# Exchanging the DMA queues of loads and stores in an attention backward kernel: paired dV and dK stores to GpSimd, K and V loads to SyncE

## The chip, the cores and the metric

One NeuronCore of a Trainium2 chip. The metric is the device time of one execution in microseconds (us). The kernel is already tuned. Its time before the change is 1880.39 us, the median of three runs (1872.74 to 1903.6). Later comparisons use runs of both kernels on the same chip in the same rounds. The record calls a run slow when it lies over 1.5% above the fastest run of the same kernel, and fast otherwise. Ratios use fast runs alone; medians are over all runs.

In the profile lines PE is TensorE, PEld its loading of weights, DVE VectorE, ACT ScalarE, POOL GpSimd and SP SyncE. A q behind an engine's name (SPq) means its sequencer, which issues its DMAs. SBUF is the on-chip memory that DMAs fill, and PSUM the one that TensorE writes, in banks. A DMA lands when its completion is reported. A ring is the queue in which one issuer's DMAs stand.

## The reference, cut to what matters

Two independent attention blocks (A and B) with cached K and V run forward and backward in one program. Each has batch 8, 96 queries, 32 heads, 512 keys and head size 128, in bfloat16. The program returns the output and the gradients of x, k_cache, v_cache, wq and wo of both blocks.

```python
q = (x @ wq).reshape(B, Sq, H, Dh).transpose(0, 2, 1, 3)
scores = einsum("bhqd,bhkd->bhqk", q, k_cache) * Dh ** -0.5
p = softmax(scores)
o = einsum("bhqk,bhkd->bhqd", p, v_cache)
out = o.transpose(0, 2, 1, 3).reshape(B, Sq, H * Dh) @ wo
# and jax.vjp of it: dx, dK, dV, dwq, dwo
```

The large data are K and V, which are read once, and dK and dV, which are written once: 512 (head, batch) pairs in all, 128 KB each for K, V, dK and dV.

## The kernel before

A software pipeline runs one (head, batch) pair, a "tick", at a time. K and V arrive for two ticks at once. V is also needed transposed (VT). A transposing DMA from SBUF to SBUF makes it. dV and dK leave PSUM through ScalarE, one tick at a time, into three SBUF buffers each, and SyncE stores them.

```python
OFF = dict(ld=-1, vt=1, s1=2, s2=3, s3=3, s4=4, s5=5, s6=7, s7=8, s8=9)   # stage -> tick

def c_ld(h, b):          # every second tick: 256 KB of V, 256 KB of K, issued by GpSimd
    K_sb = kvp.tile([128, 2, KC, 128], BF16, name="K_sb", bufs=7)
    V_sb = kvp.tile([128, 2, KC, 128], BF16, name="V_sb", bufs=5)
    nc.gpsimd.dma_start(V_sb[:], vc[b:b + 2, h].rearrange("b (p c) d -> p b c d", c=KC))
    nc.gpsimd.dma_start(K_sb[:], kc[b:b + 2, h].rearrange("b (p c) d -> p b c d", c=KC))

def c_vt(h, b):          # every second tick: 256 KB, SBUF to SBUF, issued by SyncE
    VT = kvp.tile([128, 2 * KC, 128], BF16, name="VT", bufs=4)
    nc.sync.dma_start_transpose(VT[:], CS[(blk, h, b)]["V2"][:].rearrange("p a c d -> p (a c d)"))

def c_s4(h, b):          # every tick; c_s7 does the same for dK
    dV_ps = bank([128, KC * 128], F32, "dV_ps")
    ...                  # four matmuls
    dV_sb = wk.tile([128, KC * 128], BF16, name="dV_sb", bufs=3)
    nc.scalar.activation(dV_sb[:], dV_ps[:], ACT.Identity, scale=1.0)
    nc.sync.dma_start(dv[b, h].rearrange("(p c) d -> p (c d)", c=KC), dV_sb[:])
...
ps=P(name="ps", bufs=8, space=PSUM)      # eight PSUM banks, shared by all
stp=P(name="stp", bufs=5)                # staging of block B's inputs
```

GpSimd also computes (P_sb and prod, once a tick each) and issues the DMAs of the weights and their gradients.

Of the kernel before, what the change touches and what calls it, by code (L numbers as in the profile page):

```python
# [53 lines left out]
def build_block(tc, em, tick0, blk, x, kc, vc, wq, wo, g_all, out_all, dx, dk, dv, dwq, dwo, ident, ones, pools, HG=8, first=True, groups=None):  # L54
    nc = tc.nc
# [40 lines left out]

    S = {}
    G = {}
    HS = pools["HS"]
    CS = pools["CS"]  # L100

# [127 lines left out]
    def c_ld(h, b):  # L229
        def f():  # L230
            K_sb = kvp.tile([128, 2, KC, 128], BF16, name="K_sb", bufs=7)
            V_sb = kvp.tile([128, 2, KC, 128], BF16, name="V_sb", bufs=5)
            nc.gpsimd.dma_start(V_sb[:], vc[b:b + 2, h].rearrange("b (p c) d -> p b c d", c=KC))
            nc.gpsimd.dma_start(K_sb[:], kc[b:b + 2, h].rearrange("b (p c) d -> p b c d", c=KC))  # L234
            for i in range(2):
                CS[(blk, h, b + i)] = dict(K_sb=K_sb[:, i], V_sb=V_sb[:, i], V2=V_sb)
        return f
# [104 lines left out]
    def c_s4(h, b):  # L342
        def f():
            st = CS[(blk, h, b)]
            hs = HS[(blk, h)]
            P_sb = st["P_sb"]
            dV_ps = bank([128, KC * 128], F32, "dV_ps")
            for c in range(KC):
                nc.tensor.matmul(dV_ps[:, c * 128:(c + 1) * 128], P_sb[:, c * 128:(c + 1) * 128], hs["dOnat_h"][:, b * 128:(b + 1) * 128], start=True, stop=True)  # L349
            dV_sb = wk.tile([128, KC * 128], BF16, name="dV_sb", bufs=3)  # L350
            nc.scalar.activation(dV_sb[:], dV_ps[:], ACT.Identity, scale=1.0)  # L351
            nc.sync.dma_start(dv[b, h].rearrange("(p c) d -> p (c d)", c=KC), dV_sb[:])
        return f

    def c_s5b(h, b):
        def f():
            st = CS[(blk, h, b)]
            hs = HS[(blk, h)]
            tok = slice(b * Sq, (b + 1) * Sq)
            prod = wk.tile([128, Sq], BF16, name="prod", bufs=4)  # L360
            nc.gpsimd.tensor_tensor(prod[:], hs["OT_h"][:, tok], hs["dOT_h"][:, tok], op=ALU.mult)  # L361
            st["prod"] = prod
        return f
# [13 lines left out]
    def c_s7(h, b):  # L377
        def f():
            st = CS[(blk, h, b)]
            hs = HS[(blk, h)]  # L380
            dS_sb = st["dS_sb"]
            dK_ps = bank([128, KC * 128], F32, "dK_ps")
            for c in range(KC):
                nc.tensor.matmul(dK_ps[:, c * 128:(c + 1) * 128], dS_sb[:, c * 128:(c + 1) * 128], hs["Qnat_h"][:, b * 128:(b + 1) * 128], start=True, stop=True)  # L384
            dK_sb = wk.tile([128, KC * 128], BF16, name="dK_sb", bufs=3)
            nc.scalar.activation(dK_sb[:], dK_ps[:], ACT.Identity, scale=1.0)  # L386
            nc.sync.dma_start(dk[b, h].rearrange("(p c) d -> p (c d)", c=KC), dK_sb[:])
        return f

    def qA(h, which):  # L390
# [97 lines left out]
    for g in range(NG):  # L488
        h0 = GH0[g]
        for hh in range(groups[g]):  # L490
            h = h0 + hh
            c0t = tick0 + h * B
            em.add(c0t + HK["pA"], SL_LOAD, pA(h))
            em.add(c0t + HK["pB"], SL_HEAD, pB(h))
            for si in range(NTS):
                em.add(c0t + HK["pC0"][min(si, len(HK["pC0"]) - 1)], SL_HEAD, pC(h, 0, si))
                em.add(c0t + HK["pC1"][min(si, len(HK["pC1"]) - 1)], SL_HEAD, pC(h, 1, si))
            em.add(c0t + HK["pD1"], SL_HEAD, pD(h, 1))
            em.add(c0t + HK["pD0"], SL_HEAD, pD(h, 0))
            for b in range(B):  # L500
                ct = c0t + b
                if b % 2 == 0:
                    em.add(ct + OFF["ld"], SLOTS["LOAD"], c_ld(h, b))
                    em.add(ct + OFF["vt"], SLOTS["LOAD"] + 1, c_vt(h, b))
                em.add(ct + OFF["s2"], SLOTS["S2A"], c_s2a(h, b))
                em.add(ct + OFF["s2"], SLOTS["S2B"], c_s2b(h, b))
                em.add(ct + OFF["s3"], SLOTS["S3A"], c_s3a(h, b))
                em.add(ct + OFF["s3"], SLOTS["S3B"], c_s3b(h, b))
                em.add(ct + OFF["s5"], SLOTS["S5B"], c_s5b(h, b))
                em.add(ct + OFF["s4"], SLOTS["S4"], c_s4(h, b))  # L510
                key = (blk, h, b)
                for table, stages in ((KD, ("s1", "s7", "s6")), (OD, ("s8", "s5", "s4"))):
                    for i, stage in enumerate(stages):
                        table.setdefault(ct + OFF[stage], [None] * 3)[i] = key
                em.add(ct + OFF["s6"], SLOTS["S6"], c_s6(h, b))
                em.add(ct + OFF["s7"], SLOTS["S7"], c_s7(h, b))
            em.add(c0t + HK["qA0"], SL_HEAD, qA(h, 0))
            for di in range(len(dsplits)):
                em.add(c0t + HK["qB"][min(di, len(HK["qB"]) - 1)], SL_HEAD + 1, qB(h, di))
            em.add(c0t + HK["qA1"], SL_HEAD, qA(h, 1))  # L520
            qd_parts = HK["qD"]
            for (k_, c_lo, c_hi) in qd_parts:
                if c_lo < DC:
                    em.add(c0t + k_, SL_HEAD + 2, qD(h, c_lo, min(c_hi, DC)))
        cLg = tick0 + (h0 + groups[g] - 1) * B + B - 1
        gs0 = max(3, (GSPREAD0 * groups[g]) // HG)
        gs1 = max(3, (GSPREAD1 * groups[g]) // HG)
        em.add(cLg + OFF["s5"] - 2, SL_LOAD, gW(g))
        subs = [(0, t, gi) for t in range(TT) for gi in range(len(gsplits))] + [(1, t, gi) for t in range(TT) for gi in range(len(gsplits))]
        n_out = TT * len(gsplits)  # L530
        for i, (which, t, gi) in enumerate(subs):
            if which == 0:
                tk = cLg + OFF["s5"] + 2 + (i * gs0) // n_out
            else:
                tk = cLg + OFF["s8"] + 2 + gs0 - 3 + ((i - n_out) * gs1) // n_out
            em.add(tk, SL_GRP, gU(g, which, t, gi))
# [5 lines left out]
def _kernel_impl(tc, A_x, A_k_cache, A_v_cache, A_wq, A_wo, B_x, B_k_cache, B_v_cache, B_wq, B_wo, grad_out,  # L542
           out_0, out_1, out_2, out_3, out_4, out_5, out_6, out_7, out_8, out_9, out_10, HG=8, slots=None, off=None, hk=None, ev=None, gspread=None, groupsA=None, groupsB=None):
    global GSPREAD0, GSPREAD1
    nc = tc.nc
    if slots:
        SLOTS.update(slots)
    if off:
        OFF.update(off)
    if hk:  # L550
        HK.update(hk)
    if ev:
        EV.update(ev)
    if gspread:
        GSPREAD0, GSPREAD1 = gspread
    with ExitStack() as ctx:
        P = lambda **kw: ctx.enter_context(tc.tile_pool(**kw))
        cst = P(name="gconst", bufs=1)
        ident = cst.tile([128, 128], BF16, name="ident")
        make_identity(nc, ident[:])  # L560
        ones = cst.tile([128, 1], BF16, name="ones")
        nc.vector.memset(ones[:], 1.0)
        pools = dict(
            const=P(name="const", bufs=1),
            ps=P(name="ps", bufs=8, space=PSUM),
            kvp=P(name="kv", bufs=11),
            wk=P(name="wk", bufs=3),
            hd=P(name="hd", bufs=2),
            hst=P(name="hst", bufs=HG + 2),
            grp=P(name="grp", bufs=1),  # L570
            stp=P(name="stp", bufs=5),
        )
        pools["KD"] = {}
        pools["OD"] = {}
        pools["HS"] = {}
        pools["CS"] = {}
        em = Emitter()
        t_next = 13
        for blk, args in enumerate(((A_x, A_k_cache, A_v_cache, A_wq, A_wo, grad_out, out_0, out_1, out_2, out_3, out_4, out_5),
                                    (B_x, B_k_cache, B_v_cache, B_wq, B_wo, grad_out, out_0, out_6, out_7, out_8, out_9, out_10))):  # L580
            H_ = args[1].shape[1]
            if blk == 0:
                grps = groupsA
            else:
                grps = groupsB
            t_next = build_block(tc, em, t_next, blk, *args, ident, ones, pools, HG=HG, first=(blk == 0), groups=grps)
        for tk, ks in pools["KD"].items():
            em.add(tk, SLOTS["KD"], pools["c_kd"](*ks))
        for tk, ks in pools["OD"].items():
            em.add(tk, SLOTS["OD"], pools["c_od"](*ks))  # L590
        em.run()
# [64 lines left out]
```

## Time and profile before

| what | before |
|---|---|
| span of the profiled run | 1901.0 us |
| TensorE busy / idle | 1772.6 / 128.4 us |
| ScalarE waiting for dV and dK stores | 135.1 us, 86 times |
| GpSimd waiting to issue a K load | 307.4 us |
| bytes read / written, HBM | 171.57 / 159.12 MB |

The profiled run is slow (1902.77 us).

First come the engine line and the queue lines of the page. The engine line gives busy us, share of the span and instruction count. The queue lines give packets, MB and the time that the packets took. q1 is SyncE's queue with hardware-made descriptors, q0 is GpSimd's with descriptors made in software.

```profile
PE 1772.6 (93%) x24696; PEld 1473.5 (78%) x24696; DVE 1371.5 (72%) x2803; ACT 1420.5 (75%) x4041; POOL 1151.0 (61%) x1890
...
q1 hardware_dynamic: 419360, 203.39, 58.5%
q0 software_dynamic: 60832, 194.57, 42.9%
```

Next is the view of waits. Each line says which engine and line waited for whom, then total us, number of times, and longest wait.

```profile
POOL K_sb L234 <- PE od_ps L326: 307.4, 209, 3.5
...
ACT dV_sb L351 <- DMA out_dram<-dV_sb: 84.2, 58, 5.2
...
ACT dK_sb L386 <- DMA out_dram<-dK_sb: 50.9, 28, 5.7
...
PE kd_ps L256 <- ACT dK_sb L386: 33.2, 18, 5.6
...
PE dK_ps L384 <- ACT dV_sb L351: 19.2, 15, 3.1
...
PE od_ps L330 <- POOL P_sb L309: 12.6, 46, 2.0
```

This is a chain of three. A store has not landed, so ScalarE has no SBUF buffer to evict (copy) the PSUM bank into. The PSUM bank is not freed, and TensorE waits for a bank.

Last is the DMA view, by transfer, with issuer, count, size and median us from issue to landing.

```profile
out_dram<-dV_sb SPq DMA_DIRECT2D x512, 128.0 KB, 6.3
out_dram<-dK_sb SPq DMA_DIRECT2D x512, 128.0 KB, 5.8
V_sb<-in_A_v_cache_dram POOLq DMA_DIRECT2D x128, 256.0 KB, 7.5
K_sb<-in_A_k_cache_dram POOLq DMA_DIRECT2D x128, 256.0 KB, 6.0
...
out_dram<-dwo_sb POOLq DMA_DIRECT2D x64, 160.0 KB, 7.0
...
VT<-V_sb SPq DMA_TRANSPOSE x256, 8.5
```

What one stall looks like is in the timelines of SyncE, ScalarE and TensorE around 90 us. Columns are start us, us, what, and in brackets the idle time before it and what ended it.

```profile
85.73 7.17 SPq L242 DMA_TRANSPOSE VT<-V_sb  x1
93.00 0.53 SPq L352 DMA_DIRECT2D out_dram<-dV_sb  x1
```

```profile
93.71 0.60 ACT L386 ACTIVATE dK_sb<-dK_ps 128x512 bf16<-128x512 f32 x1 [5.69 <-DMA out_dram<-dK_sb]
```

```profile
85.48 0.39 PE L256 MATMUL kd_ps<-ident,K_sb 128*128 128x128 bf16 x4
...
88.28 0.44 PE L415 MATMUL dwo_ps<-g_nat,Onat 128*128 128x128 bf16 x5
94.35 0.58 PE L256 MATMUL kd_ps<-ident,K_sb 128*128 128x128 bf16 x4 [5.63 <-ACT dK_sb L386]
```

The store that ScalarE waited for had taken 15.1 us from issue to landing. In the meantime SyncE needed 7.17 us to issue one transpose (1.47 us at the median). After the gap the same four matmuls take 0.58 us, where they took 0.39 us before it: the granted TensorE clock is halved for a few us.

### The profile page before, as it was taken

How to read it: one execution, taken by the hardware profiler on the slowest of the kernel's cores; microseconds unless marked ns; L12 is line 12 of the kernel's file. 1: busy time of each engine (PE TensorE's matmuls, PEld its weight loads, DVE VectorE, ACT ScalarE, POOL GpSimd, SP SyncE). 2: the span in 40 equal slices, each digit the busy share in tenths (PEclk: the TensorE clock that was granted, in tenths of full speed). 3: DMA queues.
4: the chain of work that ended last, by engine and by line, in shares of the span. 5: the costliest groups of instructions: out<-in, count | busy, mean ns of one | idle time of the engine just before them, and what ended most of it. 6: DMA issues, size and time to landing. Idle time of an engine off the chain costs nothing. (4 is left out here: it accounts for less than half of the span.)

```text
span 1901.0 us, 64574 instructions
## 1 busy us (share of the span) xinstructions
PE 1772.6 (93%) x24696; PEld 1473.5 (78%) x24696; DVE 1371.5 (72%) x2803; ACT 1420.5 (75%) x4041; POOL 1151.0 (61%) x1890
## 2 busy tenths in 40 slices
PE   6899999898999999988898989998999999999998
PEld 5687788777887788867777877887778877788777
DVE  5677766777777777767766877567777787778775
ACT  5788787788668886777755978777876787768782
POOL 6566555666556665556666766456665576556655
PEclk9999999999999999999999999999999999999999
DMA  9999999999989999999999999999999999988992
GB/s 266 200 222 222 230 193 197 213 208 223 218 196 223 218 224 208 210 183 212 217 226 209 243 219 213 202 192 219 220 222 202 215 226 219 214 204 207 210 224 87
DMA packets 480503, 402.08 MB, mean 212 GB/s; under 512 B 300513, under 2 KB 433121, under 8 KB 480193
## 3 DMA queue, kind: packets, MB, share of 16 engines
q1 hardware_dynamic: 419360, 203.39, 58.5%
q0 software_dynamic: 60832, 194.57, 42.9%
q8 instruction: 193, 3.16, 0.7%
q14 instruction: 118, 0.96, 0.2%
HBM read 171.57 MB, written 159.12 MB: 174 GB/s over the span
## 5 line engine op out<-in xcount | busy, mean ns | idle before, releaser
L290 ACT ACTIVATE E_sb<-S_ps,negm 96x512 bf16<-96x512 f32 x512 | 350.5, 685 | 205.7 <-DVE negm L280 198.9
L373 DVE SCALAR_TENSOR_TENSOR dS_sb<-dP_ps,kd_ps,P_sb 96x512 bf16<-96x512 f32 x512 | 383.7, 749 | 143.6 <-PE dP_ps L371 136.5
L309 POOL TENSOR_SCALAR P_sb<-E_sb,rinv 96x512 bf16<-96x512 bf16 x512 | 356.1, 696 | 197.5 <-DVE rinv L300 187.3
L280 DVE TENSOR_REDUCE negm<-S_ps 96x1 f32<-96x512 f32 x512 | 347.6, 679 | 80.0 <-PE S_ps L278 75.7
L351 ACT ACTIVATE dV_sb<-dV_ps 128x512 bf16<-128x512 f32 x512 | 313.3, 612 | 102.1 <-DMA out_dram<-dV_sb 84.2
L386 ACT ACTIVATE dK_sb<-dK_ps 128x512 bf16<-128x512 f32 x512 | 303.6, 593 | 89.4 <-DMA out_dram<-dK_sb 50.9
L268 DVE COPY kd_sb<-kd_ps 128x896 bf16<-128x896 bf16 (+2 forms) x518 | 315.4, 609 | 72.8 <-PE kd_ps L266 71.4
L335 ACT ACTIVATE PT_sb<-od_ps 128x384 bf16<-128x384 bf16 x512 | 252.3, 493 | 0.0
L256 PE MATMUL kd_ps<-ident,K_sb 128*128 128x128 bf16 x2048 | 200.8, 221 | 36.6 <-ACT dK_sb L386 33.2
L361 POOL TENSOR_TENSOR prod<-OT_h,dOT_h 128x96 bf16<-128x96 bf16 x512 | 187.6, 366 | 72.7 <-ACT OT_h L332 68.4
L384 PE MATMUL dK_ps<-Qnat_h,dS_sb 96*128 96x128 bf16 x2048 | 198.3, 219 | 21.1 <-ACT dV_sb L351 19.2
L234 POOL DMA_DIRECT2D K_sb<-in_B_k_cache_dram x128 | 97.0, 757 | 183.9 <-PE od_ps L326 156.0
L278 PE MATMUL S_ps<-kd_sb,QT_h 128*96 128x512 bf16 x512 | 197.0, 385 | 12.0 <-ACT dV_sb L351 4.9
L349 PE MATMUL dV_ps<-dOnat_h,P_sb 96*128 96x128 bf16 x2048 | 200.8, 221 | 7.9 <-ACT dV_sb L351 7.5
L256 PEld LDWEIGHTS <-K_sb 128*128 128x128 bf16 x2048 | 148.4, 99 | 66.9 <-issue 41.5
L371 PE MATMUL dP_ps<-VT,dOT_h 128*96 128x512 bf16 x512 | 198.3, 387 | 1.2 <-ACT dV_sb L351 1.1
L234 POOL DMA_DIRECT2D K_sb<-in_A_k_cache_dram x128 | 96.8, 756 | 167.7 <-PE od_ps L326 151.4
L330 PE MATMUL od_ps<-ident,P_sb 96*128 96x96 bf16 x2048 | 173.8, 207 | 13.0 <-POOL P_sb L309 12.6
L261 PE MATMUL kd_ps<-ident,dS_sb 96*128 96x96 bf16 x2048 | 174.0, 207 | 3.7 <-DVE dS_sb L373 3.2
L322 PE MATMUL od_ps<-kd_sb,K_sb 128*128 128x96 bf16 x2048 | 173.6, 207 | 2.9 <-ACT dV_sb L351 1.0
L326 PE MATMUL od_ps<-PT_sb,V_sb 128*128 128x96 bf16 x2048 | 172.5, 207 | 0.0
L300 DVE RECIPROCAL rinv<-rowsum 96x1 f32<-96x1 f32 x512 | 79.2, 155 | 102.5 <-ACT E_sb L290 96.5
(85 smaller groups left out, 4160.0 us busy)
## 6 DMA issues: line engine op xcount, KB each, us to landing
out_dram<-dV_sb SPq DMA_DIRECT2D x512, 128.0 KB, 6.3
out_dram<-dK_sb SPq DMA_DIRECT2D x512, 128.0 KB, 5.8
V_sb<-in_A_v_cache_dram POOLq DMA_DIRECT2D x128, 256.0 KB, 7.5
K_sb<-in_A_k_cache_dram POOLq DMA_DIRECT2D x128, 256.0 KB, 6.0
K_sb<-in_B_k_cache_dram POOLq DMA_DIRECT2D x128, 256.0 KB, 6.1
V_sb<-in_B_v_cache_dram POOLq DMA_DIRECT2D x128, 256.0 KB, 7.7
out_dram<-dwo_sb POOLq DMA_DIRECT2D x64, 160.0 KB, 7.0
out_dram<-dwq_sb POOLq DMA_DIRECT2D x64, 160.0 KB, 6.6
```

The costliest lines, as they stand in the source:

```text
L256: nc.tensor.transpose(kd_ps[:, c * 128:(c + 1) * 128], st["K_sb"][:, c, :], ident[:])
L268: nc.vector.tensor_copy(kd_sb[:, lo:hi], kd_ps[:, lo:hi])
L280: nc.vector.tensor_reduce(negm[:], S_ps[:], axis=AX.X, op=ALU.max, negate=True)
L290: nc.scalar.activation(E_sb[:], st["S_ps"][:], ACT.Exp, bias=st["negm"][:], scale=1.0, accum_out=rowsum[:])
L309: nc.gpsimd.tensor_scalar(P_sb[:], st["E_sb"][:], st["rinv"][:], 0.0, op0=ALU.mult, op1=ALU.add)
L335: nc.scalar.activation(PT_sb[:], PT_ps, ACT.Identity, scale=1.0)
L349: nc.tensor.matmul(dV_ps[:, c * 128:(c + 1) * 128], P_sb[:, c * 128:(c + 1) * 128], hs["dOnat_h"][:, b * 128:(b + 1) * 128], start=True, s ...
L351: nc.scalar.activation(dV_sb[:], dV_ps[:], ACT.Identity, scale=1.0)
L371: nc.tensor.matmul(dP_ps[:], hs["dOT_h"][:, tok], st["VT"], start=True, stop=True)
L373: nc.vector.scalar_tensor_tensor(dS_sb[:], dP_ps[:], st["dl_ps"], st["P_sb"][:], op0=ALU.subtract, op1=ALU.mult)
L384: nc.tensor.matmul(dK_ps[:, c * 128:(c + 1) * 128], dS_sb[:, c * 128:(c + 1) * 128], hs["Qnat_h"][:, b * 128:(b + 1) * 128], start=True, s ...
L386: nc.scalar.activation(dK_sb[:], dK_ps[:], ACT.Identity, scale=1.0)
```

## The change

The intent is to take the stores off the ring that also carries the transposes, to halve their number, and to keep GpSimd from waiting in order for the release of a K buffer. The room for two pairs of each of dV and dK comes from the input staging, cut from five to four buffers.

```diff
-            nc.gpsimd.dma_start(V_sb[:], vc[b:b + 2, h].rearrange(...))
-            nc.gpsimd.dma_start(K_sb[:], kc[b:b + 2, h].rearrange(...))
+            nc.sync.dma_start(V_sb[:], vc[b:b + 2, h].rearrange(...))
+            nc.sync.dma_start(K_sb[:], kc[b:b + 2, h].rearrange(...))
 ...
-            dV_sb = wk.tile([128, KC * 128], BF16, name="dV_sb", bufs=3)
-            nc.scalar.activation(dV_sb[:], dV_ps[:], ACT.Identity, scale=1.0)
-            nc.sync.dma_start(dv[b, h].rearrange("(p c) d -> p (c d)", c=KC), dV_sb[:])
+            if b % 2 == 0:
+                SB[(blk, h, "v")] = wk.tile([128, 2, KC * 128], BF16, name="dV_sb", bufs=2)
+            nc.scalar.activation(SB[(blk, h, "v")][:, b % 2], dV_ps[:], ACT.Identity, scale=1.0)
 ...                      # the same for dK
+    def c_st(h, b, which):
+        def f():
+            dst = dv if which == "v" else dk
+            nc.gpsimd.dma_start(dst[b - 1:b + 1, h].rearrange("b (p c) d -> p b (c d)", c=KC), SB.pop((blk, h, which))[:])
+        return f
 ...                      # emitted one tick after the second eviction, where b is odd
-            stp=P(name="stp", bufs=5),
+            stp=P(name="stp", bufs=4),
```

The order of instructions on TensorE, VectorE and ScalarE stays the same but for a handful at the start.

More of the change, by code (lines that the diff above doesn't have):

```diff
@@ L98, in build_block @@
     G = {}
+    SB = {}
     HS = pools["HS"]
@@ L232, in f @@
             V_sb = kvp.tile([128, 2, KC, 128], BF16, name="V_sb", bufs=5)
-            nc.gpsimd.dma_start(V_sb[:], vc[b:b + 2, h].rearrange("b (p c) d -> p b c d", c=KC))
-            nc.gpsimd.dma_start(K_sb[:], kc[b:b + 2, h].rearrange("b (p c) d -> p b c d", c=KC))
+            nc.sync.dma_start(V_sb[:], vc[b:b + 2, h].rearrange("b (p c) d -> p b c d", c=KC))
+            nc.sync.dma_start(K_sb[:], kc[b:b + 2, h].rearrange("b (p c) d -> p b c d", c=KC))
             for i in range(2):
@@ L384, in f @@
                 nc.tensor.matmul(dK_ps[:, c * 128:(c + 1) * 128], dS_sb[:, c * 128:(c + 1) * 128], hs["Qnat_h"][:, b * 128:(b + 1) * 128], start=True, stop=True)
-            dK_sb = wk.tile([128, KC * 128], BF16, name="dK_sb", bufs=3)
-            nc.scalar.activation(dK_sb[:], dK_ps[:], ACT.Identity, scale=1.0)
-            nc.sync.dma_start(dk[b, h].rearrange("(p c) d -> p (c d)", c=KC), dK_sb[:])
+            if b % 2 == 0:
+                SB[(blk, h, "k")] = wk.tile([128, 2, KC * 128], BF16, name="dK_sb", bufs=2)
+            nc.scalar.activation(SB[(blk, h, "k")][:, b % 2], dK_ps[:], ACT.Identity, scale=1.0)
         return f
@@ L509, in build_block @@
                 em.add(ct + OFF["s5"], SLOTS["S5B"], c_s5b(h, b))
+                if b % 2 == 1:
+                    em.add(ct + OFF["s4"] + 1, SLOTS["LOAD"], c_st(h, b, "v"))
+                    em.add(ct + OFF["s7"] + 1, SLOTS["LOAD"], c_st(h, b, "k"))
                 em.add(ct + OFF["s4"], SLOTS["S4"], c_s4(h, b))
```

## The prediction

> **What bounds the kernel now.** TensorE: 1772.6 of 1901.0 us busy (93%, page part 1), and the chain that ended last is TensorE work. About 128 us are idle, some 20 of them start-up. The 20 us windows show a base of 19.5 to 20 us busy, broken by dips to 13-17 us, often with a granted clock of 0.83 to 0.91 in the same window. In the dips the cause is mostly ScalarE: it waited 84.2 us (58 times, dV) and 50.9 us (28 times, dK) for the store that still held its SBUF buffer, up to 5.7 us at once. TensorE then waits for a PSUM bank: kd_ps on dK 33.2, dK_ps on dV 19.2, q_ps 8.9, dV_ps 7.5, S_ps 4.9 us (view of waits). Together some 75 us, plus what the lowered clock after a dip costs. GpSimd's late P_sb costs another 12.6 us.
>
> A store must leave within three ticks (slack about 9.5 us, median, from eviction end to the third next eviction); from eviction end to landing takes 6.8 (dV) and 6.1 us (dK) median, but 12 at the 95th percentile. In 1024 chances about 100 miss. Most misses have landings of 8-14 us (congestion), a third also an issue over 1.5 us late, behind a transpose on the SyncE queue.
>
> **What the change does.**
> - Arithmetic and the order on TensorE, VectorE and ScalarE stay (a handful of rows differ at the start).
> - 1024 stores of 128 KB become 512 of 256 KB on GpSimd; 512 loads of 256 KB go to SyncE. GpSimd's count of DMAs hardly changes, about 0.75 us each as for the loads: its 1151 us busy should stay within 5%.
> - GpSimd no longer waits in order for the release of K_sb (307 us, 209 times); it waits for finished evictions instead, so P_sb comes a little earlier.
> - Only every second eviction can wait (512 chances, not 1024). Slack of a pair: 9.4 us median from the second eviction's end to refill; placing the new stores after their GpSimd predecessors in the old trace gives an issue lag of 0 (dV) to 0.7 us (dK). But a 256 KB transfer on the software queue lands in 6.0-7.7 us today, and dwo's stores of 160 KB take 7.0.
> - Stores leave the ring that holds transposes, but now queue behind wo, wq, dwo, dwq, wo_r (1.28 MB) and the second block's inputs. Bytes are the same. The Trainium skill ("DMA: Bandwidth & Descriptors", issuing engines are not separate DMA queues) says all issuers share 16 DMA engines; the trace agrees: landings of both queues stretch together when transposes are in flight. So congestion stays.
> - Loads behind transposes have several ticks of prefetch; I expect no new wait for K, V or VT beyond a few us.
>
> **Sum.** ScalarE's store waits: from 135 to about 80 us (half the chances, each somewhat likelier). TensorE gets back 30 us at most of that, P_sb 5-10, start-up some us (x and g no longer share with K and V loads), less a few us lost behind wo_r. Net about -25 us.
>
> **Predicted: 1855 us, 1815 to 1893 in 8 of 10. Faster by over 2% 0.33, within 2% 0.60, slower 0.07.**
>
> **Right if** TensorE busy stays near 1770 and idle falls to about 100 us; ScalarE's store waits fall to 50-100 us with under 70 cases; GpSimd's wait for K_sb is gone; landings of stores 6-8 us median; SyncE waits for K/V releases without anyone waiting for it.
>
> **Wrong if** software stores land much faster (3-5 us: waits vanish, about 1815) because their larger packets win against the hardware queue; or slower than 9 us, or GpSimd blocks on stores and delays P_sb (over 1900); or loads in order behind transposes arrive late (TensorE waiting for K_sb, VT).

## The result, and the profile after

The changed kernel takes 1784.67 us (median of 4 runs, 1781.13 to 1789.79), and the kernel before 1887.41 us in the same comparison. The ratio is 0.9482, with a 95% interval of 0.9408 to 0.9557. A ratio here is the mean time of one kernel's fast runs over that of the other's of the same rounds, so it is not quite the ratio of the quoted medians. The change is faster by 5.2%. 1.3% was predicted, and the time lies below the stated range.

The engine and queue lines of the changed kernel:

```profile
PE 1726.8 (97%) x24547; PEld 1453.2 (81%) x24696; DVE 1370.3 (77%) x2803; ACT 1414.9 (79%) x4041; POOL 1146.2 (64%) x1890
...
q1 hardware_dynamic: 411168, 203.36, 56.0%
q0 software_dynamic: 60832, 194.57, 36.8%
```

Its waits that answer to those shown before:

```profile
POOL P_sb L310 <- DVE rinv L301: 307.3, 249, 4.7
...
ACT dK_sb L394 <- DMA out_dram<-dK_sb: 10.7, 2, 9.2
...
PE od_ps L331 <- POOL P_sb L310: 7.2, 4, 5.3
...
ACT dV_sb L353 <- DMA out_dram<-dV_sb: 3.7, 3, 1.8
```

And its DMA view:

```profile
out_dram<-dV_sb POOLq DMA_DIRECT2D x256, 256.0 KB, 4.8
out_dram<-dK_sb POOLq DMA_DIRECT2D x256, 256.0 KB, 3.7
V_sb<-in_A_v_cache_dram SPq DMA_DIRECT2D x128, 256.0 KB, 5.0
K_sb<-in_A_k_cache_dram SPq DMA_DIRECT2D x128, 256.0 KB, 3.8
...
out_dram<-dwo_sb POOLq DMA_DIRECT2D x64, 160.0 KB, 3.8
...
VT<-V_sb SPq DMA_TRANSPOSE x256, 5.9
```

ScalarE's store waits fell from 135.1 to 14.4 us (10.7 + 3.7), 86 cases to 5. TensorE's idle time (span less busy) fell from 128.4 to 56.5 us. Its busy time fell by 45.8 us at the same work. Some 10 us of this may be only records that the later trace lacks (24547 matmuls of 24696; an estimate, 0.6% of the busy time), and the idle time is then that much too large. Another part is the clock: stretches at half clock went from 17 with 71.5 us to 4 with 26.2 us. If half of such a stretch counts as lost, that is some 23 us (an estimate from those two sums). GpSimd's wait for K_sb (307.4 us before) is gone; that its wait for rinv, an input of P_sb, is now 307.3 us (187.3 before) is a coincidence of numbers.

The DMA view is the surprise. The stores land sooner although each is twice as large. So do nearly all other streams (not wo_h of block A, 5.2 us in both, nor the small stores of ob), among them the store of dwo (7.0 to 3.8 us), whose size, queue and issuer did not change. The same bytes moved, and most of the congestion went away. Which part of the change did that is the question for the experiments.

### The profile page after: what moved, and what is told of

It reads as the page before. It is cut to its first block, busy times and chain, and to the rows that moved or that the text cites. A ratio compares the mean times of both kernels' runs of the same rounds, so it can differ in the third digit from the quotient of the medians.

```text
span 1783.3 us, 62453 instructions
## 1 busy us (share of the span) xinstructions
PE 1726.8 (97%) x24547; PEld 1453.2 (81%) x24696; DVE 1370.3 (77%) x2803; ACT 1414.9 (79%) x4041; POOL 1146.2 (64%) x1890
## 5 line engine op out<-in xcount | busy, mean ns | idle before, releaser
L310 POOL TENSOR_SCALAR P_sb<-E_sb,rinv 96x512 bf16<-96x512 bf16 x512 | 354.1, 692 | 314.3 <-DVE rinv L301 307.3
L359 POOL DMA_DIRECT2D out_dram<-dK_sb x256 | 197.4, 771 | 88.6 <-ACT OT_h L333 81.6
L359 POOL DMA_DIRECT2D out_dram<-dV_sb x256 | 189.5, 740 | 6.5 <-DMA out_dram<-ob 2.3
L442 PEld LDWEIGHTS <-x_nat 128*128 128x128 bf16 x1920 | 125.6, 99 | 28.3
```

What stands on the lines that cost most here:

```text
L310: nc.gpsimd.tensor_scalar(P_sb[:], st["E_sb"][:], st["rinv"][:], 0.0, op0=ALU.mult, op1=ALU.add)
L359: nc.gpsimd.dma_start(dst[b - 1:b + 1, h].rearrange("b (p c) d -> p b (c d)", c=KC), SB.pop((blk, h, which))[:])
```

## The experiments

The theories at the start were these.

- **Route**: the stores were slow because they shared the SyncE ring with the transposes.
- **Depth**: ScalarE merely ran out of buffers, and the stalls bunched the DMAs.
- **Pairing**: half as many stores do it.
- **GpSimd's order**: its 307 us of waiting for K_sb is what cost.

Theory A, that software-queue loads beside transposes are slow, was formed after the first four runs.

| run | loads | stores | transposes | us, median | ratio | transposes land, us |
|---|---|---|---|---|---|---|
| before | GpSimd | SyncE, single | yes | 1887.41 | 1 | 8.5 |
| the change | SyncE | GpSimd, pairs | yes | 1784.67 | 0.948 | 5.9 |
| e1 | GpSimd | SyncE, single, 4 buffers | yes | 1893.06 | 0.993 | 8.7 |
| e2 | GpSimd | SyncE, pairs | yes | 1822.39 | 0.958 | 6.3 |
| e3 | SyncE | SyncE, single | yes | 1769.07 | 0.931 | 4.7 |
| e4 | GpSimd | GpSimd, pairs | yes | 2039.13 | 1.063 | 10.1 |
| e5 | SyncE | SyncE, pairs | yes | 1766.54 | 0.945 | 4.9 |
| e6 | ScalarE | SyncE, single | yes | 1803.06 | 0.966 | 4.7 |
| e7 | GpSimd | SyncE, single | copies | 1761.76 | 0.942 | (4.0) |
| e8 | SyncE | SyncE, single | copies | 1758.80 | 0.941 | (3.4) |
| e9 | V SyncE, K GpSimd | SyncE, single | yes | 1775.11 | 0.940 | 5.1 |
| e10 | K SyncE, V GpSimd | SyncE, single | yes | 1774.31 | 0.939 | 5.0 |
| e11 | SyncE | GpSimd, pairs | copies | 1765.24 | 0.935 | (4.5) |
| e12 | SyncE | GpSimd, single | yes | 1776.11 | 0.942 | 5.5 |

Ratios of different calls are each against the kernel before on that chip, whose own runs spread from 1856 to 1910 us, so compare medians within a call. The calls were e1 to e4, e5 to e8, e9 to e12, e13, and e14 to e16. The medians of e1, e2 and e4 and of the kernel before include slow runs. The record's verdict on e5 to e8 is "unclear": only two of the seven runs of the kernel before were fast on that chip. But the slowest run of e5 to e8 took 1814.01 us and the fastest of the kernel before 1855.89 us, so that the four are faster is not in doubt, only by how much.

### e1: depth alone

```diff
-dV_sb = wk.tile(..., name="dV_sb", bufs=3)      # and dK_sb
+dV_sb = wk.tile(..., name="dV_sb", bufs=4)
-stp=P(name="stp", bufs=5)
+stp=P(name="stp", bufs=4)
```

> The kernel before with only the depth changed: four single dV and four dK buffers (the bytes of the two pairs), input staging 5 to 4 buffers; same queues, single stores. Depth theory (ScalarE only ran out of buffers; each stall bunches the DMAs after it, so the long landings are a result of the stalls): ScalarE's store waits under 25 us, store landings fall from 6 to 4.5 us, ratio to before about 0.95 to 0.96. Route theory (stores are slow because they share the SyncE ring with transposes): waits fall only by half, landings stay at 6 us or more, ratio 0.975 to 0.99.

Measured: 1893.06 us, ratio 0.9928 (0.986 to 0.9997). The waits in its trace, in the same columns as above:

```profile
ACT dV_sb L351 <- DMA out_dram<-dV_sb: 73.2, 32, 10.4
...
ACT dK_sb L386 <- DMA out_dram<-dK_sb: 40.8, 20, 5.2
```

The same SBUF spent on depth leaves 114 of 135 us of waits, and the landings stay where they were (6.5 and 6.0 us). Waits are fewer but longer. Depth falls as a theory.

### e2: pairs alone

```diff
-nc.gpsimd.dma_start(dst[b - 1:b + 1, h]..., SB.pop(...)[:])
+nc.sync.dma_start(dst[b - 1:b + 1, h]..., SB.pop(...)[:])
 # and the K and V loads stay on nc.gpsimd
```

> Pairs alone: stores in pairs with two buffers, but on the SyncE queue; K and V loads stay on GpSimd. Pairing or depth theory: 0.95 to 0.965 of before, store landings about 4.5 us. Route theory: 0.98 to 1.01, landings of 256 KB stores 7 us and more, since they still queue with the transposes.

Measured: 1822.39 us, ratio 0.958 (0.953 to 0.963). Pairs help by themselves while the loads are still on GpSimd. The store waits are 31.7 and 28.8 us. Stores of twice the size land in 4.5 us. A store is issued within 0.03 us of its eviction in 95% of the cases; before, the 95th percentile was 3.0 us (dV) and 2.0 us (dK). GpSimd still waits 297.4 us for K_sb, so this gain did not need the end of that wait. The route theory, which expected 0.98 and more, is wrong here.

### e3: loads alone

```diff
-nc.gpsimd.dma_start(V_sb[:], ...)
-nc.gpsimd.dma_start(K_sb[:], ...)
+nc.sync.dma_start(V_sb[:], ...)
+nc.sync.dma_start(K_sb[:], ...)
```

> Loads alone: K and V loads move to SyncE, the single stores stay there too, behind loads that wait for a release and behind transposes. Theory that GpSimd's in-order wait for K_sb (307 us) is what costs: 0.96 to 0.98 of before. Route and depth theories: slower than before, 1.02 to 1.15, since each store may sit behind a load that waits; SyncE's waits then show up as store lag.

Measured: 1769.07 us, ratio 0.9314 (0.9283 to 0.9345), which is better than the whole change. All theories but one expected a loss, and that one (GpSimd's order) a smaller gain, 0.96 to 0.98. The DMA view:

```profile
out_dram<-dV_sb SPq DMA_DIRECT2D x512, 128.0 KB, 3.4
out_dram<-dK_sb SPq DMA_DIRECT2D x512, 128.0 KB, 3.6
...
V_sb<-in_A_v_cache_dram SPq DMA_DIRECT2D x128, 256.0 KB, 4.0
...
VT<-V_sb SPq DMA_TRANSPOSE x256, 4.7
```

The single stores are still in one ring with all the transposes, and with the loads as well. They land in 3.4 to 3.6 us, and one single wait of 2.9 us for a store is left. Sharing a ring with transposes is not what made stores slow, so the route theory falls.

### e4: stores alone

```diff
 # the changed kernel, with the loads as before:
-nc.sync.dma_start(V_sb[:], ...)     # and K_sb
+nc.gpsimd.dma_start(V_sb[:], ...)
```

> Stores alone: pairs on GpSimd, K and V loads left on GpSimd as well. Route theory: stores free of the transposes but in one ring with the loads, GpSimd busy up by about 390 us (512 issues of 0.75 us): 0.96 to 0.99. Theory that GpSimd has to be free: P_sb comes late (TensorE waits for P_sb over 40 us instead of 13), 1.00 to 1.05. Depth theory: 0.95 to 0.97.

Measured: 2039.13 us, ratio 1.0627 (1.0543 to 1.0712). The profiled run was slow. With loads and stores on the software queue, transposes land in 10.1 us and stores in 6.6 to 6.8 us. ScalarE waits 226.4 us for stores, and TensorE waits 69.3 us for P_sb. The stores' half of the change, by itself, is a clear loss, larger than any theory had expected (1.05 at most). After these four runs theory A was formed: what counts is the traffic that the software queue carries beside the transposes, loads above all.

### e5: everything on SyncE

```diff
 # the changed kernel, with its paired stores on SyncE:
-nc.gpsimd.dma_start(dst[b - 1:b + 1, h]..., SB.pop(...)[:])
+nc.sync.dma_start(dst[b - 1:b + 1, h]..., SB.pop(...)[:])
```

> The changed kernel with its paired stores put back on SyncE: K and V loads, stores and transposes all on SyncE. Theory A (software loads moving beside transposes are slow for both, the loads' move is the whole gain, GpSimd stores only cost): 1755 to 1775 us, 0.925 to 0.935 of before, no slower than the loads-alone run (0.931). Theory B (the stores' move adds a part of its own in the full change): slower than the full change, over 0.955.

Measured: 1766.54 us (1760.76 to 1769.93), ratio 0.9445 (0.932 to 0.9571). The time is as theory A expected. The ratio is not in its range, because the kernel before ran from 1856 us on that chip. The last three runs settle the comparison.

### e6: loads on a hardware ring of their own

```diff
-nc.gpsimd.dma_start(V_sb[:], ...)    # and K_sb
+nc.scalar.dma_start(V_sb[:], ...)
```

> The kernel before with the K and V loads issued by ScalarE instead of GpSimd: hardware descriptors, but a ring of their own beside that of the transposes. Theory A1 (loads of the software queue are what is slow): DMA landings fall as in the loads-alone run (stores about 3.5 us, transposes about 4.7 us) and rate in the stretches with loads and transposes is well over 212 KB/us; time 0.94 to 0.98, since 512 issues of some 0.4 us now take ScalarE's sequencer. Theory A2 (any second ring beside the transposes does it, a single ring in order avoids it): landings stay at 6 us (stores) and 8 us (transposes), time 0.99 to 1.05.

Measured: 1803.06 us, ratio 0.9656 (0.9518 to 0.9794). The DMA view:

```profile
out_dram<-dV_sb SPq DMA_DIRECT2D x512, 128.0 KB, 4.0
out_dram<-dK_sb SPq DMA_DIRECT2D x512, 128.0 KB, 3.8
V_sb<-in_A_v_cache_dram ACTq DMA_DIRECT2D x128, 256.0 KB, 3.8
...
VT<-V_sb SPq DMA_TRANSPOSE x256, 4.7
```

The loads run in a second ring beside that of the transposes, as before, but with hardware-made descriptors. Landings are about those of e3, not those of before. So a second ring is not the matter, and the software queue is. The rate that was expected to be well over 212 KB/us was not clearly so: in slices counted as under e13 below it is about 230 KB/us beside ScalarE's loads, against about 215 beside software loads in the kernel before. The time is 34 us over that of e3 (another chip). ScalarE's sequencer now spends 220.9 us in issuing 512 loads; how the 34 us divide was not traced further.

### e7 and e8: copies in place of the transposes

Both give a wrong result (VT holds V untransposed, so dP and what follows are wrong). The bytes of this stream stay.

```diff
-nc.sync.dma_start_transpose(VT[:], V2[:].rearrange("p a c d -> p (a c d)"))
+nc.sync.dma_start(VT[:], V2[:].rearrange("p a c d -> p (a c) d"))
```

> Gives a wrong result on purpose (dP, and with it dK, dQ, dx, dwq): the kernel before with every transposing DMA replaced by a plain SBUF to SBUF copy of the same bytes. Theory A (transposes beside software loads): store landings fall to 3 to 4 us, waits vanish, 1750 to 1790 us. Theory C (the transposes have no part; software loads or GpSimd's in-order wait for K_sb are slow by themselves): 1840 us or more, landings over 5 us.

> Wrong on purpose in the same way: the loads-alone kernel with the plain copy in place of the transposes. Theory A: 1745 to 1775 us, the same within 1% as the kernel before with the copy. Theory C: some 5% faster than that one.

Measured: the kernel before with copies takes 1761.76 us (ratio 0.9422), and the loads-alone kernel with copies 1758.80 us (0.9408). The kernel before thus gains all but 3 us without a single queue moved. Its waits hold one case of 0.6 us for a store of dK and none for dV. Its DMA view:

```profile
VT<-V_sb SPq DMA_DIRECT2D x256, 256.0 KB, 4.0
out_dram<-dV_sb SPq DMA_DIRECT2D x512, 128.0 KB, 3.7
out_dram<-dK_sb SPq DMA_DIRECT2D x512, 128.0 KB, 3.2
...
V_sb<-in_A_v_cache_dram POOLq DMA_DIRECT2D x128, 256.0 KB, 4.8
```

GpSimd still waits for K_sb in this run, and the loads are still software loads:

```profile
POOL K_sb L234 <- PE od_ps L326: 304.5, 221, 3.1
```

So neither costs much by itself: software loads beside copies cost 3 us (e7 against e8), and transposes without software loads some 10 us (e3, 1769.07 us, against e8; other chips). The large loss takes both the transposes and the software loads. One rival is left by these two runs: the copies may also be cheaper for the DMA engines than the transposes, so that there is merely more to spare. e13 tests that.

### e9 and e10: half of the loads

```diff
-nc.gpsimd.dma_start(V_sb[:], ...)    # e9; in e10 K_sb instead
+nc.sync.dma_start(V_sb[:], ...)
```

> The kernel before with only the V loads moved to SyncE (64 MB), K loads left on GpSimd. If what counts is how many bytes the software queue loads beside transposes: about half to three quarters of the loads-alone gain, 0.945 to 0.97 of before, transposes landing in 5 to 7 us (8.5 before, 4.7 with both moved). If it is GpSimd's wait for K_sb, which stays on GpSimd here: 0.985 to 1.01.

> The mirror: only the K loads move to SyncE, V loads stay on GpSimd. Bytes alone: the same as the V-only run within 1%. GpSimd's wait for K_sb as the cause: nearly the whole gain, 0.93 to 0.945. If the V loads matter more, because they are issued nearer to the transposes: smaller gain than the V-only run by over 1%.

Measured: 1775.11 us (0.9399) for V and 1774.31 us (0.9385) for K. The two agree, as was expected if bytes alone count, so it is not which tensor. V alone keeps GpSimd's wait for K_sb and gains as much, which clears that wait again:

```profile
POOL K_sb L234 <- PE od_ps L326: 315.0, 231, 3.1
```

(In e10 the wait is not gone either: GpSimd waits 354.5 us for V_sb instead.) Half the bytes bring nearly all of the gain, a little more than the 0.945 to 0.97 that e9 had expected for bytes: the loss does not grow in step with the bytes.

### e11 and e12: what the stores on GpSimd do in the change

```diff
 # e11: the changed kernel with copies in place of the transposes (wrong on purpose)
 # e12: the kernel before with the queues exchanged, without pairs
-nc.sync.dma_start(dv[b, h]..., dV_sb[:])     # and dk
+nc.gpsimd.dma_start(dv[b, h]..., dV_sb[:])
```

> Wrong on purpose (dP and what follows): the changed kernel with plain copies in place of the transposes. If the software stores of the changed kernel also pay for running beside transposes (and this is why it is slower than the loads-alone kernel): 1755 to 1768 us, landings of stores under 4 us. If its stores on GpSimd cost by GpSimd's order or issue time: it stays at 1775 to 1790 us.

> The exchange of queues without pairs: 1024 single stores of 128 KB on GpSimd with three buffers, loads on SyncE. If pairing is needed for the stores on GpSimd (issue time doubles to some 512 x 0.6 us more, GpSimd over 80% busy): 1.0 to 1.03 of before by late P_sb. If pairing matters little: 0.945 to 0.965, near the full change.

Measured: e11 takes 1765.24 us (0.9349), about 20 us less than the changed kernel with transposes (1785 us, another chip). Some 10 us of that come with the copies anyway (e3 against e8), so the software stores' share is an estimate of some 10 us. Their landings are 4.2 (dV) and 3.1 us (dK), so the expected 4 us was missed for dV. e12 takes 1776.11 us (0.9416), a little better than expected and not slower than the changed kernel on the other chips: once the loads are off the software queue, pairing the stores on GpSimd is not needed.

### e13: the DMA streams by themselves

No compute: streams of 16 transfers of 256 KB in the kernel's own shapes, with a full stop between phases, the list of phases run twice.

```diff
-(all of the kernel's pipeline)
+for i in range(16):
+    nc.sync.dma_start_transpose(VT[i][:], src[i][:].rearrange("p a c d -> p (a c d)"))
+    nc.gpsimd.dma_start(ld[i][:], k_cache[b:b + 2, h].rearrange("b (p c) d -> p b c d", c=4))
+barrier()          # VectorE touches every tile; then the next phase, with another issuer or stream
```

> Wrong on purpose: no compute at all, only DMA streams of the kernel's own shapes, 16 of 256 KB each, phase after phase with a full stop between, the list of 14 phases twice. Phases: transposes; software loads; ScalarE loads; software stores; ScalarE stores; transposes beside each of these four; transposes and loads in turn on SyncE; transposes with software loads and ScalarE stores (as before); transposes with software stores and ScalarE loads (as after); plain copies beside software loads; transposes beside software loads with rows of 2 KB. Theory A (a transpose and a software load slow each other): transposes beside software loads take longer than transposes beside ScalarE loads, software stores or loads in the SyncE ring by over 20%, and so does the as-before phase than the as-after one; plain copies beside software loads do not. Rival (the DMA engines simply have less to spare in the kernel before; the pairing itself costs nothing): those phases agree within 10%, and only order and bunching inside the kernel made the difference.

The windows of the first pass, one line for each phase: window and length, busy us of VectorE (the barrier) and of GpSimd (issuing), clock, DMA share, GB/s. In order: transposes alone; software loads alone; ScalarE loads alone; transposes beside software loads; beside ScalarE loads; beside software stores; in turn with loads on SyncE; copies beside software loads.

```profile
36.00:60.00 24.00, 11.10 (x63) 0.00 (x0) 1.00 0.92 175
64.00:80.00 16.00, 9.42 (x135) 11.41 (x16) 1.00 0.78 263
81.50:97.50 16.00, 9.75 (x144) 0.00 (x0) 1.00 0.81 263
135.50:185.10 49.60, 10.21 (x140) 11.53 (x16) 1.00 1.05 170
186.60:224.20 37.60, 10.27 (x143) 0.00 (x0) 1.00 1.07 224
227.90:269.50 41.60, 7.94 (x106) 11.59 (x16) 1.00 1.03 202
310.70:346.00 35.30, 11.31 (x144) 0.00 (x0) 1.00 1.06 238
473.10:500.20 27.10, 10.31 (x138) 11.53 (x16) 1.00 0.90 310
```

| phase (from first issue to last landing) | first pass, us | second pass, us |
|---|---|---|
| transposes alone | 23.8 | 23.7 |
| software loads alone | 16.2 | 16.1 |
| ScalarE loads alone | 15.7 | 16.1 |
| transposes + software loads | 49.4 | 47.0 |
| transposes + ScalarE loads | 37.4 | 38.6 |
| transposes + software stores | 41.5 | 41.4 |
| transposes + ScalarE stores | 36.2 | 36.6 |
| transposes + loads in turn on SyncE | 35.2 | 35.2 |
| copies + software loads | 27.0 | 27.2 |
| transposes + software loads + ScalarE stores | 60.6 | 56.9 |
| transposes + software stores + ScalarE loads | 61.2 | 58.4 |
| transposes + software loads with rows of 2 KB | 42.1 | 45.5 |

Two things stand out. Transposes and software loads at the same time take 49.4 us, where one after the other they would take 40.0 us (23.8 + 16.2): overlapping them is worse than not overlapping them. With ScalarE loads the pair takes 37.4 us, and in turn in one ring 35.2 us. The software loads alone are no slower than hardware ones (16.2 against 15.7 us). The packets tell the same: those of the transposes kept each DMA engine busy for 22.0 us when alone, 32.4 us beside software loads (65.3% of 49.6 us) and 24.0 us beside ScalarE loads (63.8% of 37.6 us). So the interference is there without the kernel around it, and it is not merely that there is less to spare. Copies alone were not run, so what the copies themselves pay beside software loads (27.0 us) is not known.

Theory A missed twice here. Beside software loads the transposes take only 14 to 19% longer than beside software stores, not over 20%. With all three streams at once the as-before and as-after phases take the same time within 3%, which is what the rival expected. Streams at full rate therefore do not show why software stores cost the kernel so much less than software loads.

A count of the packet records in the kernels themselves, in slices of half a us, gives one part of that. It takes the slices in which over 60 transpose packets started beside at least 20 KB of the software queue and under 20 KB of other data. There were some 590 such slices in the kernel before, at about 215 KB/us in all. In the changed kernel there were some 290, at about 300 KB/us. (Counts and rates shift by a few per cent with where the slices begin.) The stores there overlap the transposes less, and at a better rate.

### e14 to e16: the changed kernel and the two better ones on one chip

> The changed kernel again, beside the next two on one chip. If moving the stores to GpSimd costs about 1%: 1780 to 1790 us, and the next two 15 to 20 us faster, their ranges clear of this one's. If it is neutral: all three within 8 us.

> The loads-alone kernel on the same chip as the changed kernel. Stores' move costs: 1762 to 1775 us. Neutral: within 8 us of the changed kernel.

> Loads on SyncE and paired stores on SyncE, on the same chip. Stores' move costs: 1760 to 1772 us; pairing is worth nothing once the loads have moved, so within 6 us of the loads-alone kernel.

Measured (no edits but those of the change, e3 and e5): the changed kernel 1786.34 us (1784.99 to 1788.6, ratio 0.9462), loads alone 1767.29 us (1764.1 to 1770.83, 0.9361), loads and paired stores on SyncE 1766.16 us (1765.14 to 1766.48, 0.9353). The ranges do not overlap with that of the changed kernel. Both simpler kernels beat it by about 20 us, and pairing is worth 1 us once the loads have moved.

## Why the prediction was right or wrong

- **The bound and the chain of waits: right.** Stores late, ScalarE without a buffer, TensorE without a bank. The gain came back through exactly these waits.
- **"So congestion stays": this is the step that failed.** The prediction said that the bytes are the same and all issuers share the same engines, so store landings would stay at 6 to 8 us. The landings of nearly all streams fell instead, stores to 3.7 and 4.8 us, transposes from 8.5 to 5.9 us, and the untouched dwo stores from 7.0 to 3.8 us. The sum of bytes does not decide it. Transposes beside software loads take longer than the two one after the other (49.4 against 40.0 us, e13). The change took the K and V loads out of that combination. e3 (loads alone 0.931), e7 (no transposes, nothing moved, 0.942) and e6 (loads in a second hardware ring, low landings) show it from three sides. The prediction had the clue in hand: it saw landings stretch while transposes were in flight (in the trace before, dV stores issued during a transpose land in 6.5 us at the median, the 19 that met none in 2.5 us), and took that for plain sharing.
- **"ScalarE's store waits: from 135 to about 80 us": wrong in size, by that step.** They fell to 14.4 us. TensorE's idle time fell by 71.9 us to 56.5 us, where about 100 us were forecast.
- **The lowered clock was named and not counted.** Half-clock stretches fell from 71.5 to 26.2 us, by the estimate above some 23 us of the gain. So TensorE's busy time did not stay near 1770 us as forecast; it is 1726.8 us.
- **"Wrong if software stores land much faster ... because their larger packets win": the landings came true, the reason did not.** In e3 the stores have no larger packets and stay on the hardware queue, and they land in 3.4 to 3.6 us. The time went 30 us below the 1815 us given for this case.
- **"GpSimd's wait for K_sb is gone", its busy time within 5%, no new wait for K, V or VT, SyncE waiting at no cost: right.** GpSimd's busy time was 1151.0 and is 1146.2 us. But the end of the wait for K_sb was not needed for the gain: it stays in e2 (0.958), e7 (0.942) and e9 (0.940).
- **"A few us lost behind ... the second block's inputs" and wo_r: right in kind.** One wait of 9.2 us for a dK store is left between 918 and 942 us, where a load of 1280 KB on the same software queue took 19.3 us to land.
- **The small terms: one right, one wrong.** P_sb gave back 5.4 us (12.6 to 7.2 us; 5 to 10 were forecast). The start-up gave nothing: TensorE waited 11.8 us for x and g before and 13.1 us after.
- **Pairing as the source of the gain (half the chances): right only where it does not matter.** With the loads still on GpSimd, pairs alone give 0.958 (e2). With the loads moved they give 1 us (e15 and e16).

What the Trainium skill says and the prediction leaned on is in "DMA: Bandwidth & Descriptors", section "Issuing engines are not separate DMA queues": DMAs of all issuers interleave on the same 16 engines, and another issuer only saves issue time. The first half agrees with the traces, since landings of all queues rise and fall together. The second half does not hold for this mix: the same loads from another issuer changed the time by 6.9% (e3). The prediction read it as "who issues does not change the congestion", and that reading was the error. The rule of the same page to coalesce small transfers ("Rules for kernel authors") sees mostly overhead under 64 KB. The single stores here have 128 KB, so this does not test it; pairing them was worth 1 us once the loads had moved (1767.29 us with single stores, 1766.16 us with pairs).

Left open are three things. The mechanism inside a DMA engine by which a transpose and a software load slow each other is not seen in these traces. A rival within it was not tested by itself: by the packet records software loads go in packets of 4096 bytes and those of SyncE and ScalarE in packets of 1024, with 256 for transposes, so the size of the packets and not the queue may be what counts. Rows of 2 KB in the software loads, in packets of the same size, shortened the phase from 49.4 and 47.0 to 42.1 and 45.5 us, so the shape of a load matters too. Why stores suffer less than loads in the kernel, but not with three full streams, is only partly answered by their smaller overlap. And whether e2's gain comes from the earlier issue or from the halved number of chances was not separated.

## What to carry to other kernels

When every transfer's landing time is long while the bytes per second are well below what the same core reaches elsewhere in the trace, look for two kinds of traffic that hinder each other, and take one kind out as a test (here: copies for transposes, with a wrong result) before redesigning buffers. Where transposing DMAs run all the time, try the big loads on a hardware queue, even in the same ring as everything else. Change one queue at a time: here the half that looked like a helper was the whole gain, and the half that looked like the point cost 1% on top of it (and 6% by itself).

## What the Trainium skill lacked or had wrong

- "DMA: Bandwidth & Descriptors" says that the issuing engine only saves sequencer time, and of a transpose next to ordinary DMAs that it "needs nothing". That may hold for correctness, but for speed the page lacks this: 16 transposes of 256 KB beside 16 loads from GpSimd took 49.4 and 47.0 us, beside the same loads from ScalarE 37.4 and 38.6 us, in turn with loads from SyncE 35.2 us, and one after the other they would take 40.0 us.
- The same page gives a transposing DMA 261 GB/s in one case and 350 to 400 GB/s when contiguous. Here, SBUF to SBUF and alone, 16 of 256 KB took 23.8 us, 176 GB/s. SyncE was issuing for 20.9 us of this, so whether the issuing or the moving sets this rate is not shown.
- The same page calls the time to issue a DMA usually small relative to the DMA. A transpose took SyncE 1.23 us at least, 1.47 us at the median and 10.66 us at most in the kernel before, and whatever stood behind it in SyncE's order waited.
- No page tells how the loss grows with the software loads: taking half of them away brought ratios of 0.940 and 0.939 (e9, e10), taking all of them 0.931 and 0.936 (e3, e15).
